# One planner's rule for transfers behind a row of single words, wider weight chunks, and a bound in bfloat16

## The chip, the cores and the metric

The kernel runs on one core of one Trainium2 chip. What counts is the device time of one execution in microseconds, the median of several executions of the same program. The core has five instruction queues that run side by side, each strictly in its own order: PE (matmuls), DVE (vector), ACT (scalar), POOL (GpSimd) and SP, which here issues all the DMAs. An instruction that waits for a semaphore holds up everything behind it on its queue.

## The reference

Attention of many tokens to few pooled keys, and then a feed-forward layer with the gate h − tanh(h). The keys are pooled 4 × 4 and serve as the values too:

```python
B, N, C = q.shape                       # 4, 12288, 128
kv_pool = kv.reshape(B, H // r, r, W // r, r, C).mean(axis=(2, 4))   # 96 x 8 places: 768 keys a batch
k = v = kv_pool.reshape(B, -1, C) @ w_sr
s = scale * (q @ k.transpose(0, 2, 1))
a = np.exp(s - s.max(-1, keepdims=True))
x = (a / (a.sum(-1, keepdims=True) + 1e-09)) @ v
h = x.reshape(B * N, C) @ w_in          # w_in: 128 x 2048, float64
g = h - np.tanh(h)
out = g @ w_out                         # w_out: 2048 x 128, float64
```

## The kernel before

**Precision.** Nearly all matmuls run in float16, and an operand that needs more bits is split into a high and a low half: `qh`/`ql`, `vt` (two parts), `a` (two parts), `x` (two parts), `wih`/`wil`, `woh`/`wol`, `gh`/`gl`. The float64 weights arrive as pairs of 32-bit words and are turned into float32 by bit operations on DVE and ACT.

**Groups and units.** The 49152 tokens are worked on in 96 groups of 512 tokens (24 to a batch). Attention of a group, `attention(g, …)`, goes through four tiles of 128 tokens. Per tile: six matmuls give the scores `s` (L695), DVE takes the largest, `nm` (L703), ACT the exponential `e` with its sum (L709) and the high half of `a` (L714), POOL the low half (L717), and SP transposes both halves by a DMA into `at` (L721). When all four sums are there, DVE makes their inverse `inv` (L734); `store_row` (L738) writes these 512 numbers to DRAM as single 4-byte words, and `load_row` (L742) reads them back spread over all partitions as `row`; SP waits for the store's landing before that load. Groups 0 and 1 make their row on PE. The values' product `x` (L774, 18 matmuls in six steps) needs all four transposes. DVE then divides by `row` (L787) and splits `x` (L794); a store `xs` of x goes out for a rarely taken other branch.

The feed-forward layer of a group has eight units. Per unit PE computes `h` (`forth`, L814 to L816, six matmuls of 512 columns), ACT tanh and a square (L842, L845), DVE `gg` (L848), POOL `gh` (L852), DVE `gl` (L859), and PE adds to `acc` (`fro`, L820 to L822, six matmuls). After eight units ACT scales `acc` into `o` (L881) and SP stores it (L884). PE works on the scores of one group, the values of the one before it and the units of an earlier one in turn.

**What sets the order.** No engine's order is written out. Every instruction is given to the class `Plan` with a step (a place in the sequence), an engine, an estimated time, and what it reads and writes; `Plan.run` then goes through time, always starts the instruction that can begin first (or, among those that can begin within `SOON`, the one with the lowest step), and the order so found is the order in the program. `SHIFT` moves all instructions of a kind by some steps, `EARLY` whole parts. The estimates are used in this planning only: on the chip, waits are set by semaphores. Three marks for DMAs matter here. `"rows"` is the row store, which notes when it will have landed (10 us later). `"read"` marks loads. A transpose has neither.

**Start and end.** The keys of the first batch arrive in pieces by place (`product_of_place`, L512: float32 matmuls with `wsr`); those of the later batches are pooled by DVE (L501) during the batch before. `words_of` (L303 to L346) turns the weights' words to float32 in chunks of WN = 512 columns, four chunks for each matrix; `weights_in` and `weights_out` scale and split them. The last part, `is_small`, bounds the largest h from the weights' column sums (L950: `of_m` by `aw`, four float32 matmuls of 512 columns) and sets the flag that chooses between this path and the other branch.

Of the kernel before, what the change touches and what calls it, by code (L numbers as in the profile page):

```python
# [20 lines left out]
P = 128  # L21
KB = 64
WN = 512
G = 512
# [40 lines left out]
class Plan:  # L65
# [10 lines left out]
        "divide": 0.1, "exps": -0.64, "forth": 0.58, "fro": 3.75, "g_high": 1.39, "g_low": 0.61,  # L76
        "inverse": 0.06, "largest_score": -1.25, "largest_x": -0.1, "pool": 12.74,
        "q_high": 0.33, "q_low": 0.28, "result": -0.72, "scores": 0.18, "square": -0.48,
        "store": -1.47, "store_row": 3.34, "store_x": 0.33, "tanh": -0.6, "turn_weights": 0.78,
# [42 lines left out]
    def run(self, between):  # L122
# [78 lines left out]
def attention_then_ffn(ctx: ExitStack, tc: tile.TileContext, q, kv, w_sr, w_in, w_out, out):  # L201
# [92 lines left out]
    def words_of(step, load_step, n, kind, out):  # L294
# [3 lines left out]
        sb(words, "words", [P, WN, 2], U32, 4)  # L298
        sb(ym, "ym", [P, 2, WN], F32, 2)

        def load():
            if kind == "i":
                SP.dma_start(out=plan[words], in_=w_in32[:, n * WN : (n + 1) * WN, :])  # L303
            else:
                SP.dma_start(out=plan[words].rearrange("p (t c) two -> p t c two", c=C),
                             in_=w_out32[:, n * (WN // P) : (n + 1) * (WN // P)])

# [41 lines left out]
        plan.op(load_step, "SP", 0.5, load, (), (words,), late=2.0, dma=1.3, dram="read")  # L349
        plan.op(step, "DVE", 0.36, top, (words,), (Y,), port=True)  # L350
        plan.op(step, "ACT", 0.6, size, (Y,), (M,))
        plan.op(step, "DVE", 0.7, bottom, (M, Y), (Y,), port=True)
        plan.op(step, "DVE", 0.36, shift, (Y,), (M,), port=True)
        plan.op(step, "DVE", 0.7, upper, (Y, M), (part,), port=True)
        plan.op(step, "DVE", 0.36, power, (part,), (Y,), port=True)
        plan.op(step, "DVE", 0.7, lower, (words, Y), (M,), port=True)
        plan.op(step, "POOL", 1.5, add, (part, M), (part,))

    def weights_in(step):

        wa = "wa"
        sb(wa, "at", [P, F], F32, 2)
        for n in range(NW):
            words_of(step, step - 46 + 3 * n, n, "i", (wa, slice(n * WN, (n + 1) * WN)))
        by, back = wis[:, 1:2], wis[:, 0:1]

        def largest(n):
            V.tensor_reduce(out=top4[:, n : n + 1], in_=plan[wa][:, n * WN : (n + 1) * WN],
                            op=ALU.max, axis=AX.X, apply_absolute_value=True)

        def power():
            V.tensor_reduce(out=by, in_=top4, op=ALU.max, axis=AX.X)
            power_of_two(by, back, 2.0**-100)

        def high(n):
            sl = slice(n * WN, (n + 1) * WN)
            A.activation(out=wih[:, sl], in_=plan[wa][:, sl], func=AF.Copy, scale=by)

        def low(n):
            sl = slice(n * WN, (n + 1) * WN)  # L380
            V.scalar_tensor_tensor(out=wil[:, sl], in0=plan[wa][:, sl], scalar=by, in1=wih[:, sl],
                                   op0=ALU.mult, op1=ALU.subtract)

        top4 = const.tile([P, NW], F32, name="top4")
        plan.tile("top4", "top4", 1, lambda: None)
        for n in range(NW):
            plan.op(step, "DVE", 0.67, partial(largest, n), ((wa, n * WN),), (("top4", n),))
        plan.op(step, "DVE", 0.8, power, ("top4",), ("wis",))
        for n in range(NW):
            plan.op(step, "ACT", 0.6, partial(high, n), ((wa, n * WN), "wis"), (("wih", n),))  # L390
            plan.op(step, "DVE", 0.7, partial(low, n), ((wa, n * WN), "wis", ("wih", n)),
                    (("wi", n),), port=True)

    def weights_out(step):
# [9 lines left out]
        places = [("wb.0", 0), ("wb.1", 0), ("wb.2", 0), ("wb.2", WN)][:NW]  # L404
        assert NW <= 4
# [14 lines left out]
        for n in range(NW):  # L420
# [3 lines left out]
            sb(aw, "aw", [P, WN], F32, 2)  # L424
            plan.op(step + n, "ACT", 0.62, partial(sizes, n, aw), ((key, at),), (aw,), late=0.1)
            plan.op(step + n, "PE", 1.0, partial(sums, n, aw), (aw, "ident"), ("sum.o",), late=0.2,
# [39 lines left out]
        for n in range(NW):  # L466
            key, at = places[n]
            s = step + NW + 1 + n
            plan.op(s, "DVE", 0.7, partial(scaled, n), ((key, at), "sum.o"), ((key, at),))
            plan.op(s, "ACT", 0.6, partial(high, n), ((key, at),), (("woh", n),))  # L470
            plan.op(s, "DVE", 0.7, partial(low, n), ((key, at), ("woh", n)), (("wol", n),), port=True)
            plan.op(s, "ACT", 0.6, partial(small, n), (("woh", n),), (("wo", n),))
# [17 lines left out]
    def keys(b, s0):  # L490
# [25 lines left out]
        if b:  # L516
            gap, cut = 6, 4
            sb(kvp, "kvp", [P, K], F32, 1)
            for j in range(K // KB):
# [3 lines left out]
                        dram="read", after=("unit", *divmod(int(s) - 8, UN)))  # L523
# [41 lines left out]
        def size():  # L565
            back, by = plan[vs][:, 0:1], plan[vs][:, 1:2]
            V.tensor_reduce(out=by, in_=sums(), op=ALU.max, axis=AX.XY, apply_absolute_value=True)
            power_of_two(by, back, 2.0**-80)
            V.tensor_scalar(out=back, in0=back, scalar1=1.0 / W, scalar2=None, op0=ALU.mult)
# [47 lines left out]
        plan.op(s0, "DVE", 2.0, size, (pk,), (vs, scale_q))  # L617
        plan.op(s0, "ACT", 0.92, values_high, (pk, vs), ((vt, 0),))
        plan.op(s0, "DVE", 0.95, values_low, (pk, vs, (vt, 0)), ((vt, 1),))
# [21 lines left out]
    def attention(g, s0):  # L641
# [36 lines left out]
        plan.op(s0 - 8, "SP", 0.4, load_q, (), (qs,), late=2.0, dma=0.65, dram="read")  # L678
# [85 lines left out]
        else:  # L764
# [3 lines left out]
                    dram="read")  # L768
# [40 lines left out]
        plan.op(s2 + 2, "SP", 0.5, store_x, (x2,), (f"xs.{g}",), late=2.0, dma=0.8)  # L809
# [14 lines left out]
    def feed_forward(g, s0):  # L824
# [62 lines left out]
        plan.op(s0 + UN + 2, "SP", 0.5, store, (o,), (), late=3.0, dma=0.65)  # L887
# [5 lines left out]
    def is_small(step):  # L893
        for k, shape in (("m", [P, 2]), ("of_m", [P, P]), ("tops", [P, F // G]), ("by", [P, B]),
                         ("fits", [P, B + 1])):
            sb(k, k, shape, F32, 1)
        plan.tile("stat", "stat", 1, lambda: None)
# [17 lines left out]
        def weigh():  # L915
            V.tensor_tensor(out=plan["fits"][:, 0:B], in0=stat[:, 0:B], in1=plan["by"], op=ALU.mult)
            V.tensor_reduce(out=plan["m"][:, 0:1], in_=plan["fits"][:, 0:B], op=ALU.max, axis=AX.X)
            V.tensor_scalar(out=plan["of_m"], in0=ones, scalar1=plan["m"][:, 0:1], scalar2=1.001,
# [22 lines left out]
        for n in range(F // G):  # L941
            aw, p = f"aw.{n}", f"p.{n}"
            sb(aw, "row", [P, G], F32, 2)
# [12 lines left out]
            plan.op(step + n, "PE", 1.1, total, (aw, "of_m"), (p,), late=0.2, wide=True)  # L956
# [129 lines left out]
    weights_in(-LEAD - 1 + early("weights_in", 0.0))  # L1086
# [69 lines left out]
```

## Time and profile before

| | |
|---|---|
| median of 3 runs | 2847.41 us (2844.72 to 2848.29) |
| profiled execution | 2846.34 us, its span 2844.6 us, mean granted clock 0.997 |
| PE busy | 2795.4 us, 98% of the span |
| DVE busy | 2685.2 us, 94% |
| ACT busy | 2593.7 us, 91% |
| POOL busy | 1368.2 us, 48% |
| DMA | 285 MB, mean 100 GB/s; 665168 of 736420 packets under 512 B |
| SP's waits for a row store's landing (L742) | 493.0 us in 78 waits, longest 8.3 us |

"Busy" is the time in which an engine has an instruction in work. A row such as `PE x L774 <- DMA at<-a: 9.0, 3, 5.3` reads: PE, before instructions of line 774 that write x, sat idle until DMAs from a to at had landed; 9.0 us in all, three times, 5.3 the longest. In a row for one line the numbers behind the count are the shortest, median and longest duration in ns, then the start of the first and the last in us; a line "DMA to landing" under it is the time from issue to landing. In a row of a stretch stand its bounds and length, then busy us (and instructions) of PE, PEld, DVE, ACT and POOL, the granted PE clock, the share of the DMA engines, and GB/s. A matmul's duration is longer than its distance to the next one, since matmuls overlap.

### The profile page before, as it was taken

Reading aid. Unit: us, or ns where it says so; the run is one execution under the profiler, and the core shown is the slowest. Engines: PE = TensorE matmul, PEld = TensorE weight load, DVE = VectorE, ACT = ScalarE, POOL = GpSimd, SP = SyncE. Lnnn points to the kernel's source line nnn. Section 1 sums busy time; section 2 is a strip of 40 time slices with the busy share of each in tenths; the row PEclk is TensorE's granted clock in tenths of the full one; section 3 lists DMA queues with packets and bytes.
Section 4 is the critical chain, followed back from the end, with each engine's and each line's share of the span. In section 5 each row is a group of like instructions: output and inputs, shape, how many; then the busy total and the mean of one; then the engine's idle time right before and its main releaser. Section 6 shows DMA issues by size and latency. Waiting matters only on the chain. (4 is left out here: it accounts for less than half of the span.)

```text
span 2844.6 us, 39535 instructions
## 1 busy us (share of the span) xinstructions
PE 2795.4 (98%) x13380; PEld 1318.0 (46%) x13380; DVE 2685.2 (94%) x3212; ACT 2593.7 (91%) x3307; POOL 1368.2 (48%) x1069
## 2 busy tenths in 40 slices
PE   7899999999999999999999999999999999999998
PEld 3444444444444444444444444444444444444443
DVE  7989999999999999999999999999999999999998
ACT  5989999999999999999999999999999999999986
POOL 3444544444544544444545454444444454545442
PEclk9999999999999999999999999999999999999999
DMA  8445466565444446655544544666454445444430
GB/s 231 80 81 99 88 113 111 116 119 90 97 87 100 87 99 107 119 112 118 91 97 89 97 89 100 116 115 118 98 98 86 98 87 100 87 100 86 97 78 28
DMA packets 736420, 285.01 MB, mean 100 GB/s; under 512 B 665168, under 2 KB 692944, under 8 KB 736208
## 3 DMA queue, kind: packets, MB, share of 16 engines
q1 hardware_dynamic: 736208, 282.41, 50.8%
q8 instruction: 106, 1.74, 0.4%
q14 instruction: 106, 0.87, 0.2%
HBM read 79.23 MB, written 50.52 MB: 46 GB/s over the span
## 5 line engine op out<-in xcount | busy, mean ns | idle before, releaser
L852 POOL TENSOR_SCALAR gh<-gg 128x1024 f16<-128x1024 f32 x672 | 723.7, 1077 | 1237.3 <-DVE gl L859 676.5
L848 DVE SCALAR_TENSOR_TENSOR gg<-h,by_batch,t 128x1024 f32<-128x1024 f32 x768 | 983.1, 1280 | 87.7 <-ACT t L845 31.4
L859 DVE SCALAR_TENSOR_TENSOR gl<-gh,gg 128x1024 f16<-128x1024 f16 x768 | 1005.6, 1310 | 8.0 <-POOL gh L852 2.2
L842 ACT ACTIVATE t<-h,by_batch 128x1024 f32<-128x1024 f32 x768 | 850.3, 1107 | 124.7 <-PE h L816 118.3
L845 ACT ACTIVATE t<-t 128x1024 f32<-128x1024 f32 x768 | 811.3, 1056 | 21.2
L717 POOL TENSOR_TENSOR a<-e,a 128x768 f16<-128x768 f32 x384 | 633.6, 1650 | 209.4 <-ACT t L845 84.5
L814 PE MATMUL h<-x,wih 128*128 128x512 f16 x1536 | 582.1, 379 | 13.8 <-DVE gg L848 12.6
L822 PE MATMUL acc<-gl,wos 128*128 128x512 f16 x1536 | 582.4, 379 | 0.3 <-DVE gl L859 0.3
L820 PE MATMUL acc<-gh,woh 128*128 128x512 f16 x1536 | 582.5, 379 | 0.0
L821 PE MATMUL acc<-gh,wol 128*128 128x512 f16 x1536 | 582.4, 379 | 0.0
L815 PE MATMUL h<-x,wih 128*128 128x512 f16 x1536 | 582.0, 379 | 0.2 <-DVE x L794 0.2
L816 PE MATMUL h<-x,wil 128*128 128x512 f16 x1536 | 582.0, 379 | 0.0
L774 PE MATMUL x<-at,vv 128*128 128x512 f16 x1728 | 467.8, 381 | 9.2 <-DMA at<-a 9.0
L709 ACT ACTIVATE e<-s,nm 128x768 f32<-128x768 f32 x380 | 340.3, 896 | 58.5 <-DVE nm L705 56.1
L703 DVE TENSOR_REDUCE nm<-s 128x1 f32<-128x768 f32 x380 | 361.0, 950 | 20.9 <-PE s L695 20.8
L714 ACT CAST a<-e 128x768 f16<-128x768 f32 x384 | 315.5, 822 | 3.0
L695 PE MATMUL s<-vt,qh 128*128 128x384 f16 x1520 | 311.0, 327 | 6.9 <-DVE vt L578 4.8
L774 PEld LDWEIGHTS <-vv 128*128 128x128 f16 x1728 | 169.3, 98 | 212.7 <-DMA at<-a 7.4
L814 PEld LDWEIGHTS <-wih 128*128 128x128 f16 x1536 | 150.1, 98 | 186.9 <-DVE gg L848 18.2
L815 PEld LDWEIGHTS <-wih 128*128 128x128 f16 x1536 | 150.0, 98 | 184.9 <-issue 21.8
L822 PEld LDWEIGHTS <-wos 128*128 128x128 f16 x1536 | 150.4, 98 | 181.4 <-issue 0.5
L816 PEld LDWEIGHTS <-wil 128*128 128x128 f16 x1536 | 150.1, 98 | 181.7 <-issue 0.5
(136 smaller groups left out, 1774.2 us busy)
## 6 DMA issues: line engine op xcount, KB each, us to landing
qs<-in_q_dram SPq DMA_DIRECT2D x96, 256.0 KB, 2.7
xs<-x SPq DMA_DIRECT2D x96, 256.0 KB, 2.4
out_dram<-o SPq DMA_DIRECT2D x96, 256.0 KB, 2.4
row<-sums_row SPq DMA_DIRECT2D x94, 256.0 KB, 4.5
kc<-in_kv_dram SPq DMA_DIRECT2D x36, 512.0 KB, 4.4
at<-a SPq DMA_TRANSPOSE x384, 4.0
kc<-in_kv_dram SPq DMA_DIRECT2D x8, 384.0 KB, 7.4
words<-in_moe_w_in_dram SPq DMA_DIRECT2D x4, 512.0 KB, 8.4
```

The source lines that it names most:

```text
L717: return PL.tensor_tensor(out=plan[a][:, 1], in0=plan[e], in1=plan[a][:, 0], op=ALU.subtract)
L774: PE.matmul(out=plan[x], lhsT=l, rhs=r, start=(n == 0 and k == 0), stop=(n == KT - 1 and k == 2))
L814: PE.matmul(out=h, lhsT=wih[:, fs], rhs=xh, start=True, stop=False)
L815: PE.matmul(out=h, lhsT=wih[:, fs], rhs=xl, start=False, stop=False)
L816: PE.matmul(out=h, lhsT=wil[:, fs], rhs=xh, start=False, stop=True)
L820: PE.matmul(out=acc, lhsT=woh[:, fs], rhs=gh, start=(f == 0), stop=False)
L822: PE.matmul(out=acc, lhsT=wos[:, fs], rhs=gl, start=False, stop=(f == FT - 1))
L842: A.activation(out=plan[t], in_=plan[h], func=AF.Tanh, scale=node)
L845: A.activation(out=plan[t], in_=plan[t], func=AF.Square)
L848: V.scalar_tensor_tensor(out=plan[gg], in0=plan[h], scalar=weight, in1=plan[t], op0=ALU.mult, op1=ALU.mult)
L852: return PL.tensor_scalar(out=plan[gh], in0=plan[gg], scalar1=1.0 / LOW, scalar2=1.0, op0=ALU.mult, op1=ALU.mult)
L859: return V.scalar_tensor_tensor(out=plan[gl], in0=plan[gh], scalar=-LOW, in1=plan[gg], op0=ALU.mult, op1=ALU.add)
```

## The change

Five edits.

1. **The planner.** A transfer marked `"wait"` isn't started on SP before the last row store is planned to have landed. The mark is given to the loads of weights' words, keys and q, to `load_row`, and to the stores of x and of the result. Before, only loads were affected, and only by a later landing. Transposes are free of the rule in both. The tables of shifts are new.
2. **WN from 512 to 1024.** Two chunks for each weight matrix instead of four, each loaded by two DMAs of 512 KB; the ring of `words` has two buffers instead of four, all chunks of `w_out` lie in buffers of the keys (`kc`).
3. **`size` of the keys in two.** The split of `vt` needs only the first part of the key's scale.
4. **The bound in bfloat16.** `of_m` and `aw` of `is_small` become bfloat16, with a margin of 1.02 for 1.001.
5. **Keys first.** The first key tile is loaded before the first words, and all words of `w_out` behind the last keys.

```diff
-WN = 512
+WN = 1024
...
     SHIFT = {
...
-        "values": 1.09, "weight_high": 0.78, "weight_low": 0.56, "x_high": 0.78, "x_low": -7.03,
+        "values": 2.47, "weight_high": 0.78, "weight_low": 1.15, "x_high": 0.53, "x_low": -5.72,
...
-    EARLY = {"attention 0": -2.7, "attention 1": -3.6, "attention 2": -2.1, "attention 3": -5.1, "weights_in": -1.6, "weights_out": 9.5}
-    SOON = 0.184
+    EARLY = {"attention 0": -6.1, "attention 1": -4.0, "attention 2": -4.0, "attention 3": -9.3, "weights_in": -11.5, "weights_out": 12.3}
+    SOON = 0.126
...
                         held = free.get("port", 0.0) if self.ops[i][5] else 0.0
+                        if self.ops[i][8] == "wait":
+                            held = free.get("rows", 0.0)
...
             if dma:
-                landed = free.get("rows", 0.0) if dram == "read" else 0.0
-                free["dma"] = max(free.get("dma", 0.0), now + us, landed) + dma
+                free["dma"] = max(free.get("dma", 0.0), now + us) + dma
...
-        sb(words, "words", [P, WN, 2], U32, 4)
+        sb(words, "words", [P, WN, 2], U32, 2)
...
-        plan.op(load_step, "SP", 0.5, load, (), (words,), late=2.0, dma=1.3, dram="read")
-        plan.op(step, "DVE", 0.36, top, (words,), (Y,), port=True)
+        for h in range(2):
+            plan.op(load_step + 3 * h, "SP", 0.45, partial(load, h), (), ((words, h),), late=2.0,
+                    dma=1.3, dram="wait")
+        plan.op(step, "DVE", 0.7, top, (words,), (Y,), port=True)
...
-        sb("wb.0", "o", [P, WN], F32, 2)
-        sb("wb.1", "o", [P, WN], F32, 2)
-        sb("wb.2", "kc", [P, 2 * WN], F32, 5)
+        for n in range(NW):
+            sb(f"wb.{n}", "kc", [P, WN], F32, 5)
...
-        plan.op(s0, "DVE", 2.0, size, (pk,), (vs, scale_q))
-        plan.op(s0, "ACT", 0.92, values_high, (pk, vs), ((vt, 0),))
+        plan.op(s0, "DVE", 1.6, size, (pk,), (vs,))
+        plan.op(s0, "DVE", 0.35, size_by_window, (vs,), ((vs, 0), scale_q))
+        plan.op(s0, "ACT", 0.92, values_high, (pk, (vs, 1)), ((vt, 0),))
...
             plan.op(s1, "SP", 0.5, load_row, (f"dram.{g}",), (row,), late=3.2, dma=0.65,
-                    dram="read")
+                    dram="wait")
...
-        plan.op(s2 + 2, "SP", 0.5, store_x, (x2,), (f"xs.{g}",), late=2.0, dma=0.8)
+        plan.op(s2 + 2, "SP", 0.5, store_x, (x2,), (f"xs.{g}",), late=2.0, dma=0.8, dram="wait")
...
-        plan.op(s0 + UN + 2, "SP", 0.5, store, (o,), (), late=3.0, dma=0.65)
+        plan.op(s0 + UN + 2, "SP", 0.4, store, (o,), (), late=2.0, dma=0.65, dram="wait")
...
+        sb("of_m", "of_m", [P, P], BF16, 1)
...
-            sb(aw, "row", [P, G], F32, 2)
+            sb(aw, "qj", [P, G], BF16, 1)
...
-            plan.op(step + n, "PE", 1.1, total, (aw, "of_m"), (p,), late=0.2, wide=True)
+            plan.op(step + n, "PE", 0.22, total, (aw, "of_m"), (p,), late=0.2)
```

**How it moves instructions.** First SP in the start of the program, around the row store of group 3. In these rows `at<-a` is a transpose, `sums_row<-inv` the row store, `row<-sums_row` the row's load, `xs<-x` the store of x, `qs` a load of q. Before:

```order
L721 DMA_TRANSPOSE at<-a 128x12x128 x3
L742 DMA row<-sums_row 128x512
L721 DMA_TRANSPOSE at<-a 128x12x128
L802 DMA xs<-x_768 256x1x512
L721 DMA_TRANSPOSE at<-a 128x12x128
L738 DMA sums_row<-inv 128x4x1
L802 DMA xs<-x_858 256x1x512
L662 DMA qs<-in_q_dram 128x512
L742 DMA row<-sums_row 128x512
```

And after:

```order
L729 DMA_TRANSPOSE at<-a 128x12x128 x3
L750 DMA row<-sums_row 128x512
L810 DMA xs<-x_669 256x1x512
L729 DMA_TRANSPOSE at<-a 128x12x128
L746 DMA sums_row<-inv 128x4x1
L729 DMA_TRANSPOSE at<-a 128x12x128
L750 DMA row<-sums_row 128x512
L810 DMA xs<-x_757 256x1x512
```

Before, the fourth transpose of group 3 (the single one behind the first `xs<-x`) stands ahead of the group's row store. After, the row store stands between the third and the fourth.

Then SP at the first change of batch, around the row store of group 25. Before:

```order
L721 DMA_TRANSPOSE at<-a 128x12x128
L742 DMA row<-sums_row 128x512
L721 DMA_TRANSPOSE at<-a 128x12x128
L802 DMA xs<-x_7213 256x1x512
L721 DMA_TRANSPOSE at<-a 128x12x128
L662 DMA qs<-in_q_dram 128x512
L721 DMA_TRANSPOSE at<-a 128x12x128
L738 DMA sums_row<-inv 128x4x1
L721 DMA_TRANSPOSE at<-a 128x12x128
```

And after:

```order
L729 DMA_TRANSPOSE at<-a 128x12x128 x3
L810 DMA xs<-x_7131 256x1x512
L670 DMA qs<-in_q_dram 128x512
L746 DMA sums_row<-inv 128x4x1
L729 DMA_TRANSPOSE at<-a 128x12x128 x2
L892 DMA out_dram<-o 128x512
L750 DMA row<-sums_row 128x512
```

Here too the fourth transpose stood ahead of the store; after, it is the first of the two behind it. The same holds in groups 49 and 73, where the next batches begin.

DVE at the same place, from the largest score `nm` of group 25's last tile to the inverse of its sums. Before:

```order
L703 TENSOR_REDUCE nm<-s 128x1
L705 TENSOR_SCALAR nm<-nm 128x1
L798 TENSOR_REDUCE most_x<-x_7213 128x1
L859 SCALAR_TENSOR_TENSOR gl<-gh,gg 128x1024
L670 SCALAR_TENSOR_TENSOR ql<-qs,by_batch,qh 128x512
L848 SCALAR_TENSOR_TENSOR gg<-h,by_batch,t 128x1024
L734 TENSOR_REDUCE inv<-sums_all 128x4
L735 RECIPROCAL inv<-inv 128x4
```

And after:

```order
L711 TENSOR_REDUCE nm<-s 128x1
L713 TENSOR_SCALAR nm<-nm 128x1
L806 TENSOR_REDUCE most_x<-x_7131 128x1
L802 TENSOR_TENSOR x_7131<-xf,x_7131 128x512
L867 SCALAR_TENSOR_TENSOR gl<-gh,gg 128x1024 x2
L678 SCALAR_TENSOR_TENSOR ql<-qs,by_batch,qh 128x512
L856 SCALAR_TENSOR_TENSOR gg<-h,by_batch,t 128x1024 x2
L711 TENSOR_REDUCE nm<-s 128x1
L713 TENSOR_SCALAR nm<-nm 128x1
L742 TENSOR_REDUCE inv<-sums_all 128x4
L743 RECIPROCAL inv<-inv 128x4
```

x_low, a second gl, a second gg and the next tile's `nm` now stand ahead of the inverse. On PE, between the last score matmul of group 25 and its first value matmul, stood 24 matmuls of scores, 18 of values and 114 of units; after, 12, 18 and 60. In group 3 it was 6, 18 and 84; after, 15 of values, 12 of units and eight small ones of the weights' scale, and the first `fro` of the program stands behind the values of group 3 (before, ahead of them).

More of the change, by code (lines that the diff above doesn't have):

```diff
@@ L297, in words_of, with load @@
         a, at = out
-        sb(words, "words", [P, WN, 2], U32, 4)
+        sb(words, "words", [P, WN, 2], U32, 2)
         sb(ym, "ym", [P, 2, WN], F32, 2)
-        def load():
+        def load(h):
+            half = WN // 2
+            at = slice(n * WN + h * half, n * WN + (h + 1) * half)
+            to = plan[words][:, h * half : (h + 1) * half]
             if kind == "i":
-                SP.dma_start(out=plan[words], in_=w_in32[:, n * WN : (n + 1) * WN, :])
+                SP.dma_start(out=to, in_=w_in32[:, at, :])
             else:
-                SP.dma_start(out=plan[words].rearrange("p (t c) two -> p t c two", c=C),
-                             in_=w_out32[:, n * (WN // P) : (n + 1) * (WN // P)])
+                SP.dma_start(out=to.rearrange("p (t c) two -> p t c two", c=C),
+                             in_=w_out32[:, at.start // P : at.stop // P])
         def y(dt=F32):
@@ L348, in words_of, with weights_in @@
         Y, M, part = (ym, "y"), (ym, "m"), (a, at.start)
-        plan.op(load_step, "SP", 0.5, load, (), (words,), late=2.0, dma=1.3, dram="read")
-        plan.op(step, "DVE", 0.36, top, (words,), (Y,), port=True)
[L351 to L359, printed above, removed]
+        for h in range(2):
+            plan.op(load_step + 3 * h, "SP", 0.45, partial(load, h), (), ((words, h),), late=2.0,
+                    dma=1.3, dram="wait")
+        plan.op(step, "DVE", 0.7, top, (words,), (Y,), port=True)
+        plan.op(step, "ACT", 1.06, size, (Y,), (M,))
+        plan.op(step, "DVE", 1.24, bottom, (M, Y), (Y,), port=True)
+        plan.op(step, "DVE", 0.7, shift, (Y,), (M,), port=True)
+        plan.op(step, "DVE", 1.24, upper, (Y, M), (part,), port=True)
+        plan.op(step, "DVE", 0.7, power, (part,), (Y,), port=True)
+        plan.op(step, "DVE", 1.24, lower, (words, Y), (M,), port=True)
+        plan.op(step, "POOL", 2.6, add, (part, M), (part,))
+    def weights_in(step, first):
         wa = "wa"
@@ L363, in weights_in @@
         for n in range(NW):
-            words_of(step, step - 46 + 3 * n, n, "i", (wa, slice(n * WN, (n + 1) * WN)))
+            words_of(step, first + 1 + 6 * n, n, "i", (wa, slice(n * WN, (n + 1) * WN)))
         by, back = wis[:, 1:2], wis[:, 0:1]
@@ L386, in weights_in @@
         for n in range(NW):
-            plan.op(step, "DVE", 0.67, partial(largest, n), ((wa, n * WN),), (("top4", n),))
+            plan.op(step, "DVE", 1.2, partial(largest, n), ((wa, n * WN),), (("top4", n),))
         plan.op(step, "DVE", 0.8, power, ("top4",), ("wis",))
         for n in range(NW):
-            plan.op(step, "ACT", 0.6, partial(high, n), ((wa, n * WN), "wis"), (("wih", n),))
-            plan.op(step, "DVE", 0.7, partial(low, n), ((wa, n * WN), "wis", ("wih", n)),
+            plan.op(step, "ACT", 1.08, partial(high, n), ((wa, n * WN), "wis"), (("wih", n),))
+            plan.op(step, "DVE", 1.24, partial(low, n), ((wa, n * WN), "wis", ("wih", n)),
                     (("wi", n),), port=True)
@@ L403, in weights_out @@
         plan.tile("col", "col", 1, lambda: None)
-        places = [("wb.0", 0), ("wb.1", 0), ("wb.2", 0), ("wb.2", WN)][:NW]
-        assert NW <= 4
+        places = [(f"wb.{n}", 0) for n in range(NW)]
         def chunk(n):
@@ L423, in weights_out @@
             words_of(step + n, step + n - 4, n, "o", (key, slice(at, at + WN)))
-            sb(aw, "aw", [P, WN], F32, 2)
-            plan.op(step + n, "ACT", 0.62, partial(sizes, n, aw), ((key, at),), (aw,), late=0.1)
-            plan.op(step + n, "PE", 1.0, partial(sums, n, aw), (aw, "ident"), ("sum.o",), late=0.2,
+            sb(aw, "aw", [P, WN], F32, 1)
+            plan.op(step + n, "ACT", 1.08, partial(sizes, n, aw), ((key, at),), (aw,), late=0.1)
+            plan.op(step + n, "PE", 1.9, partial(sums, n, aw), (aw, "ident"), ("sum.o",), late=0.2,
                     wide=True)
@@ L468, in weights_out @@
             s = step + NW + 1 + n
[L469 to L472, printed above, removed]
+            plan.op(s, "DVE", 1.2, partial(scaled, n), ((key, at), "sum.o"), ((key, at),))
+            plan.op(s, "ACT", 1.05, partial(high, n), ((key, at),), (("woh", n),))
+            plan.op(s, "DVE", 1.2, partial(low, n), ((key, at), ("woh", n)), (("wol", n),), port=True)
+            plan.op(s, "ACT", 1.05, partial(small, n), (("woh", n),), (("wo", n),))
     plan.tile("wih", "wih", 1, lambda: None)
@@ L522, in keys @@
                 plan.op(s - 6, "SP", 0.5, partial(load, j, KB, key), (), (key,), late=2.0, dma=1.3,
-                        dram="read", after=("unit", *divmod(int(s) - 8, UN)))
+                        dram="wait", after=("unit", *divmod(int(s) - 8, UN)))
                 for k in range(cut):
```

20 lines of the change are left out of this document (11 added, 9 removed).

## The prediction

> **What bounds the kernel now.** I read the page first, then the waits of PE by stretch, the busy time by stretch, the DMA issues on SP, and last single instructions around the waits. From the page:
>
> ```profile
> span 2844.6 us, 39535 instructions
> PE 2795.4 (98%) x13380; PEld 1318.0 (46%) x13380; DVE 2685.2 (94%) x3212; ACT 2593.7 (91%) x3307; POOL 1368.2 (48%) x1069
> ...
> GB/s 231 80 81 99 88 113 111 116 119 90 97 87 100 87 99 107 119 112 118 91 97 89 97 89 100 116 115 118 98 98 86 98 87 100 87 100 86 97 78 28
> ```
>
> TensorE is the bound: 2844.6 − 2795.4 leaves 49.2 us of PE idleness, and only that can be won without taking PE work away. DVE, at 94%, is a close second. PE's waits, first up to 160 us, then in the middle from 300 to 2750 us (total us, times, longest):
>
> ```profile
> PE x L774 <- DMA at<-a: 9.0, 3, 5.3
> PE s L512 <- DMA t<-in_kv_dram: 7.7, 1, 7.7
> PE h L814 <- DVE gg L848: 5.7, 17, 0.5
> ```
>
> The third row is the whole wait of 2450 us: the middle has 5.7 us to give, about 1.9 at each of its three changes of batch. The start holds the rest, and there the values' product (L774) waits for transposed weights `at`. Busy time by stretch (each engine's busy us, then the granted clock):
>
> ```profile
> 50.00:100.00 50.00, 38.83 (x186) 19.17 (x185) 42.05 (x75) 46.57 (x79) 28.37 (x20) 0.93 0.72 132
> 100.00:150.00 50.00, 48.65 (x232) 22.43 (x230) 48.49 (x53) 44.15 (x56) 23.51 (x18) 1.00 0.35 62
> ```
>
> From 100 us on both PE and DVE are nearly full, so whatever PE loses there isn't made up later.
>
> **The row of single words.** `store_row` (L738) writes 512 single words; a transpose (L721) usually lands 4 us after its issue. Landing lines, of the row stores and then of all transposes (min/median/max):
>
> ```profile
> DMA to landing us min/median/max: 7.7/9.0/13.6
> DMA to landing us min/median/max: 3.6/4.0/11.9
> ```
>
> The long transposes are those issued just behind a row store. First group 4 (its last scores on PE, row store, transpose, first values), then a group of the steady state:
>
> ```profile
> L695 PE MATMUL s<-vt,ql x2: 326/326/326, 133.6 to 133.7; 128*128 128x384 f16 x2
> L738 SPq DMA_DIRECT2D sums_row<-inv x1: 833/833/833, 141.0 to 141.0; - x1
> L721 SPq DMA_TRANSPOSE at<-a x1: 7079/7079/7079, 144.4 to 144.4; - x1
> DMA to landing us min/median/max: 10.4/10.4/10.4
> L774 PE MATMUL x<-at,vv x3: 607/634/634, 154.9 to 155.7; 128*128 128x512 f16 x3
> ...
> L695 PE MATMUL s<-vt,ql x2: 326/326/326, 282.4 to 282.5; 128*128 128x384 f16 x2
> L738 SPq DMA_DIRECT2D sums_row<-inv x1: 389/389/389, 290.7 to 290.7; - x1
> L721 SPq DMA_TRANSPOSE at<-a x1: 1422/1422/1422, 291.9 to 291.9; - x1
> DMA to landing us min/median/max: 10.7/10.7/10.7
> ```
>
> Landings: 154.8 and 302.6, so 13.8 and 11.9 us behind the store's issue and 20.9 and 19.9 behind the end of the scores. With nothing ahead of it the same step is short, in group 3 and, at a change of batch, in group 25:
>
> ```profile
> L695 PE MATMUL s<-vt,ql x2: 326/326/326, 86.9 to 87.1; 128*128 128x384 f16 x2
> L721 SPq DMA_TRANSPOSE at<-a x1: 1435/1435/1435, 98.4 to 98.4; - x1
> DMA to landing us min/median/max: 3.7/3.7/3.7
> ...
> L721 SPq DMA_TRANSPOSE at<-a x1: 1452/1452/1452, 783.4 to 783.4; - x1
> DMA to landing us min/median/max: 3.7/3.7/3.7
> ```
>
> What matters is whether PE has other work queued between a group's last scores and its first values. I count it from PE's order: 0.22 us for a matmul of 512 columns (row of the tail below), 0.16 for one of 384. In the steady state of before that is 32.4 us, against 19.9: hidden. In group 4 it is 15.5 against 20.9, and the difference, 5.4, is the longest wait of L774, 5.3. This one place shows the whole mechanism.
>
> **Part 1, the planner.** The new rule holds loads and stores while a row is on its way, but not transposes, which are what PE waits for; a transpose is still priced at 4.75 us after its start (1.45 + 1.2 + 2.1). With the new tables the work queued on PE becomes, for groups 2 to 5, 10.2, 7.9, 14.9 and 17.5 us (before 14.2, 23.3, 15.5, 30.4); for groups 25 and 26, and likewise at the other two changes, 18.8 and 16.8 (before 32.4 both). In the steady state it stays at 24.9 or more: hidden by that work. In all of these, SP has the row store ahead of the group's last transpose (before, of these groups, only in 2, 4 and 5). The durations on DVE between a score and its row store, from the groups of 55 to 150 us:
>
> ```profile
> L848 DVE SCALAR_TENSOR_TENSOR gg<-h,by_batch,t 128x1024 f32<-128x1024 f32 x19 | 24.2, 1279 | 1.1 <-ACT t L845 0.2
> L859 DVE SCALAR_TENSOR_TENSOR gl<-gh,gg 128x1024 f16<-128x1024 f16 x17 | 21.9, 1293 | 0.2 <-POOL gh L852 0.2
> L703 DVE TENSOR_REDUCE nm<-s 128x1 f32<-128x768 f32 x14 | 13.3, 951 | 3.4 <-PE s L695 3.4
> L794 DVE TENSOR_TENSOR x<-xf,x 128x512 f16<-128x512 f32 x4 | 3.4, 853 | 0.0
> L798 DVE TENSOR_REDUCE most_x<-x 128x1 f32<-128x512 f16 x4 | 2.7, 680 | 0.5 <-ACT x L791 0.5
> L670 DVE SCALAR_TENSOR_TENSOR ql<-qs,by_batch,qh 128x512 f16<-128x512 f32 x3 | 2.3, 752 | 0.0
> L342 DVE SCALAR_TENSOR_TENSOR ym<-words,ym 128x512 f32<-128x512 uint32 x3 | 2.1, 693 | 0.1
> ```
>
> Group 3. Walking the new order with these durations I put its last scores at 88.6 (before 87.4). Then nm (1.1 with its sign), two gg (2.6) and the inverse (0.3) put the row store at about 93.5 and, 11.9 later, the transpose at 105.5. The values (18 × 0.22) and one unit's six matmuls, which now stand ahead of the first `fro`, bring that to 105.5 + 5.2 = 110.7. Without the hold, DVE would let it start at 103.6 (nm, and 13.6 us of rows up to the last `wol`). The cost is 7. The first `fro` started here before:
>
> ```profile
> L820 PE MATMUL acc<-gh,woh x1536: 376/379/634, 99.3 to 2837.3; 128*128 128x512 f16 x192
> ```
>
> 62.3 us of matmuls stand ahead of it before and 66.2 after, so PE was 37.0 us behind its work there, and would be 37.4 without the hold and 44.5 with it. Group 4: 20.9 against 14.9 instead of 15.5, +0.6. Group 5: 19.9 against 17.5, +2.4. A stall of this size also lowers the clock. After the waits of 2.5 and 5.3 us, and in an undisturbed stretch:
>
> ```profile
> PE x L774 <- DMA at<-a: 2.5, 1, 2.5
> ...
> 55.00:60.00 5.00, 4.46 (x13) 1.72 (x12) 1.55 (x5) 4.92 (x11) 4.28 (x3) 0.50 1.04 189
> 155.00:160.00 5.00, 5.00 (x15) 2.01 (x14) 2.83 (x4) 1.62 (x2) 1.64 (x1) 0.55 0.85 207
> 160.00:165.00 5.00, 5.00 (x25) 2.25 (x23) 2.89 (x3) 3.36 (x4) 0.00 (x0) 1.00 0.09 17
> ```
>
> 15 matmuls where 25 fit: 10 × 0.2 = 2.0 us, which I add once for group 5. The start: 7 + 0.6 + 2.4 + 2.0 = +12.
>
> The Trainium skill ("TensorE: Matmul & The Clock Gate", Part 1: The HAM clock gate) has the clock halved after about 3.4 us of idleness, which would spare group 5's stall and one in each batch change, some 2 us apiece; the 0.50 behind a wait of 2.5 us says otherwise, so the added 2.0 stays.
>
> Group 25. DVE now has x_low, most_x, two gl, ql, two gg and the next nm between nm and the inverse: 0.85 + 0.68 + 2.59 + 0.75 + 2.56 + 1.1 + 0.3 = 8.8, with nm itself 9.9. The store goes at about 10.8 behind the scores and the transpose lands 11.9 later, 22.7 against 18.8: +3.9. Group 26: 19.9 against 16.8, +3.1, less as DVE catches up in the first stall; I take 2. Plus one loss of clock, 2.0, minus the 1.9 that PE waited there anyway: +6 for each change of batch, +18 in all. Bounds: −5.7 (no stall, and the old waits gone) to +30.
>
> **Part 2, 1024 columns.** On DVE some 32 instructions fewer. Row L342 against row L848, twice the width: 693 × 2 − 1279 = 107 ns each, 3.4 us of DVE before the first `fro`; that is in the 103.6. **Part 3**, the split `size`: two tiny operations off the way, 0.3 us at most, inside the same wait. **Part 5, keys first**: the first key no longer queues behind 512 KB of words; at the 231 GB/s of the page's first slice that is some 2.3 us of the 7.7. But DVE now has both chunks of `wil` ahead of the first group's ql, 2 × 1.28 us (L848's width), so I leave the first scores where they are: 0, between −2.3 and 0. The words of `w_out`, now behind the last keys, come later by what two key loads take; DVE has the first groups' scores to do meanwhile.
>
> **Part 4, bound in bfloat16.** One pair of L950 in the tail's chain, and one ordinary matmul:
>
> ```profile
> 2799.88 0.22 PE acc L821
> ...
> 2823.00 0.86 PE x L950 x2
> ```
>
> Four pairs at 0.86, replaced by four matmuls at 0.22: −2.6, on PE's path (PE waits little there); between −2.6 and 0, since DVE is full up to the last gl.
>
> **Sum.** Profiled execution 2846.3 + 12 + 18 − 2.6 = 2873.7; it lies 1.1 under the median of the runs, 2847.4, so 2874.8, and with the caught-up side a little larger than I can count, 2873 (+0.9%).
>
> **Rivals.** (a) Faster: in the new places the transpose isn't held, or lands early enough. For it: in group 2 of before the transpose is issued 4.5 us behind the store, which lands 8.8 us after its own issue, and PE doesn't wait, so a store that goes early costs less; and DVE, not PE, may pace both places.
>
> ```profile
> L738 SPq DMA_DIRECT2D sums_row<-inv x1: 399/399/399, 76.3 to 76.3; - x1
> ...
> L721 SPq DMA_TRANSPOSE at<-a x1: 2659/2659/2659, 80.8 to 80.8; - x1
> ```
>
>  Then the waits of 5.3 with its 2.0 of clock and the tail go: 2846.3 − 7.3 − 2.6 + 1.1 = 2837.5. It decides if the transposes of groups 3 and 25 land under 14 us after their scores. Against it stand both landings above 10 us. Here the Trainium skill ("DMA: Bandwidth & Descriptors", Queues, rings and completion order) speaks for (a): data descriptors carry no barrier, and a later transfer may finish before an earlier one; by that the time would be (a)'s, and landings of 10.4 and 10.7 against 3.7 disagree. (b) The start stalls, the changes of batch don't, since DVE's extra pooling gives PE's queue its own delay: 2846.3 + 12 − 2.6 + 1.1 = 2857. (c) The change doesn't do what it says: what the rule holds back on SP was hidden before and is now, and new stalls equal the old ones: 2843 to 2852.
>
> **How the numbers follow.** Forecast 0.45 (own range 2862 to 2888: batch changes at +3 to +10), (a) 0.27, (b) 0.17, (c) 0.11. A measurement here can tell 0.2% from no change (2841.7 to 2853.1). Faster 0.27, same 0.11, slower 0.62. The range runs from (a), 2837, to the forecast's upper end, 2888; about 0.1 is left out on each side.
>
> **What would show it.** Right: PE waits at the values for `at` near 100, 130 to 160, 770 and 800 us, and likewise 700 us later twice; transposes of 10 us and more behind row stores there; the granted clock low right behind; first `fro` at 108 or later. The first key's wait near 5.7 and the first scores no earlier; the bound's matmuls four at 0.22. Wrong: PE's waits for `at` under 9 us in all, first `fro` before 104, or PE full from 750 to 850. What I trust least is the walk of DVE up to 88.6 and 22.7: each us there moves the sum by one, or three.

## The result

The changed kernel took 2876.14 us in the median of four runs (2875.07 to 2876.76), the kernel before 2846.73 beside it: a ratio of 1.0107, 95% interval 1.0093 to 1.012. It is slower, by 29.4 us. First the page of the changed kernel:

```profile
span 2874.8 us, 39147 instructions
PE 2803.3 (98%) x13375; PEld 1315.6 (46%) x13376; DVE 2672.0 (93%) x3180; ACT 2584.6 (90%) x3295; POOL 1382.0 (48%) x1065
```

The span grew by 30.2 us. PE's idleness went from 49.2 to 71.5 us, and PE's busy time rose by 7.9 although it has four matmuls fewer to do. Part of that is a slower clock: the mean granted clock of the two profiled executions is 0.995 against 0.997. Another part is waiting that doesn't show as idleness. Here are both kernels from the first `forth` of group 11 to that of group 78, before and after, with the same number of matmuls and the clock at 1.00 in both:

```profile
398.00:2327.70 1929.70, 1923.06 (x9266) 905.46 (x9265) 1850.45 (x2228) 1793.91 (x2282) 943.09 (x737) 1.00 0.54 102
408.40:2358.00 1949.60, 1929.92 (x9266) 904.14 (x9265) 1856.12 (x2228) 1788.48 (x2279) 949.65 (x738) 1.00 0.54 101
```

Of the 19.9 us that this stretch is longer, 13.0 are idleness and 6.9 are busy time. A matmul of 512 columns is in work for 379 ns and the next one starts 216 ns after it, so a gap shorter than the difference counts as busy. In this stretch PE starts a unit's or a score's first matmul 0.1 to 0.3 us late 61 times in the changed kernel (11.3 us in all) and 21 times before (4.3). DVE and ACT each have less to do over the whole program (13 and 9 us). PE's waits, up to 170 us, then up to 2780, then the rest:

```profile
PE x L782 <- DMA at<-a: 9.7, 3, 4.5
PE s L703 <- ACT qh L675: 6.8, 1, 6.8
PE s L703 <- ACT e L717: 5.6, 6, 2.0
PE s L516 <- DMA t<-in_kv_dram: 5.3, 1, 5.3
PE x L782 <- issue: 5.2, 1, 5.2
...
PE h L822 <- DVE gg L856: 7.0, 22, 0.7
PE x L782 <- DMA at<-a: 6.0, 4, 1.7
PE acc L830 <- DVE gl L867: 4.0, 3, 1.4
...
PE h L822 <- DVE gg L856: 2.5, 2, 1.6
PE acc L828 <- POOL gh L860: 1.6, 2, 1.4
PE acc L830 <- DVE gl L867: 1.5, 3, 0.7
```

L782 is the values' product (L774 before), L703 the scores, L830 the last part of `fro`. A fourth row of the second block, `x <- gl` with 1.3 us in one wait, is left out here. Apart from its waits for gg the second block is new: the kernel before had 6.3 us of waits for gg there and 0.2 for x. A row with `issue` names no releaser; the one of 5.2 us stands ahead of the values of group 4, whose last transpose was issued 1.6 us behind the row store. Followed group by group (the first `forth` of each), the changed kernel is 10.4 us behind at group 11, 16.5 at group 30, 23.7 at group 54 and 30.3 at group 78; its end is 30.2 behind. The loss arises in the start and around the three changes of batch.

The places that the prediction named, in order of time: group 3's last scores, its row store, its fourth transpose, its first values; then the row store, the transpose and the first values of group 25:

```profile
L703 PE MATMUL s<-vt,ql x2: 527/528/528, 88.0 to 88.3; 128*128 128x384 f16 x2
L746 SPq DMA_DIRECT2D sums_row<-inv x1: 394/394/394, 92.7 to 92.7; - x1
L729 SPq DMA_TRANSPOSE at<-a x1: 1287/1287/1287, 93.8 to 93.8; - x1
L782 PE MATMUL x<-at,vv x8: 607/634/635, 101.0 to 104.0; 128*128 128x512 f16 x8
...
L746 SPq DMA_DIRECT2D sums_row<-inv x1: 370/370/370, 764.8 to 764.8; - x1
L729 SPq DMA_TRANSPOSE at<-a x1: 1457/1457/1457, 766.3 to 766.3; - x1
L782 PE MATMUL x<-at,vv x6: 377/378/379, 775.4 to 776.4; 128*128 128x512 f16 x6
```

Both transposes sit behind a row store, and the values start 8.3 and 10.6 us after that store's issue. Group 25's wait of 1.3 us stands under `x <- gl` in the profile; it goes with the 16-byte stores below, so it is counted here as a wait for the transpose. The granted clock (last but two columns) behind the wait in group 3, and at the batch change:

```profile
100.00:105.00 5.00, 4.01 (x10) 1.49 (x11) 5.00 (x5) 3.60 (x4) 0.00 (x0) 0.50 0.26 49
755.00:760.00 5.00, 3.65 (x18) 1.60 (x17) 4.93 (x8) 4.90 (x7) 0.58 (x1) 1.00 0.55 125
775.00:780.00 5.00, 4.64 (x23) 2.27 (x24) 3.66 (x4) 4.49 (x7) 2.52 (x2) 1.00 0.75 184
```

It falls to half with a wait of 4.5 us, and stays at 1.00 with those of 1.1 to 1.4 us.

### The profile page after: what moved, and what is told of

Same layout as the page of the kernel before. It is cut to its first block, busy times and chain, and to the rows that moved or that the text cites. A ratio compares the mean times of both kernels' runs of the same rounds, so it can differ in the third digit from the quotient of the medians.

```text
span 2874.8 us, 39147 instructions
## 1 busy us (share of the span) xinstructions
PE 2803.3 (98%) x13375; PEld 1315.6 (46%) x13376; DVE 2672.0 (93%) x3180; ACT 2584.6 (90%) x3295; POOL 1382.0 (48%) x1065
## 5 line engine op out<-in xcount | busy, mean ns | idle before, releaser
L860 POOL TENSOR_SCALAR gh<-gg 128x1024 f16<-128x1024 f32 x672 | 738.9, 1100 | 932.9 <-DVE gl L867 353.5
L853 ACT ACTIVATE t<-t 128x1024 f32<-128x1024 f32 x768 | 811.4, 1057 | 22.4
L822 PE MATMUL h<-x,wih 128*128 128x512 f16 x1536 | 582.2, 379 | 12.6 <-DVE gg L856 10.2
L830 PE MATMUL acc<-gl,wos 128*128 128x512 f16 x1536 | 582.7, 379 | 5.6 <-DVE gl L867 5.6
L782 PE MATMUL x<-at,vv 128*128 128x512 f16 x1728 | 463.7, 382 | 22.3 <-DMA at<-a 15.6
L703 PE MATMUL s<-vt,qh 128*128 128x384 f16 x1520 | 310.3, 327 | 12.9 <-ACT qh L675 6.8
L782 PEld LDWEIGHTS <-vv 128*128 128x128 f16 x1728 | 169.5, 99 | 224.7 <-issue 21.2
L828 PEld LDWEIGHTS <-woh 128*128 128x128 f16 x1536 | 150.5, 98 | 185.2 <-issue 8.0
L822 PEld LDWEIGHTS <-wih 128*128 128x128 f16 x1536 | 150.1, 98 | 185.5 <-DVE gg L856 18.3
L830 PEld LDWEIGHTS <-wos 128*128 128x128 f16 x1536 | 150.4, 98 | 181.6 <-issue 0.6
```

Source lines behind the costliest of these rows:

```text
L782: PE.matmul(out=plan[x], lhsT=l, rhs=r, start=(n == 0 and k == 0), stop=(n == KT - 1 and k == 2))
L822: PE.matmul(out=h, lhsT=wih[:, fs], rhs=xh, start=True, stop=False)
L828: PE.matmul(out=acc, lhsT=woh[:, fs], rhs=gh, start=(f == 0), stop=False)
L830: PE.matmul(out=acc, lhsT=wos[:, fs], rhs=gl, start=False, stop=(f == FT - 1))
L853: A.activation(out=plan[t], in_=plan[t], func=AF.Square)
L860: return PL.tensor_scalar(out=plan[gh], in0=plan[gg], scalar1=1.0 / LOW, scalar2=1.0, op0=ALU.mult, op1=ALU.mult)
```

## The experiments

Theory A: transposes are held by the row of single words, and the new order leaves PE too little else at those places. Theory B: the new order itself costs PE the time, whatever a store takes. Theory C: the wide chunks or the keys' order cost the start. The twelve runs, each with the kernel before on the same chip; lines with the same time of before belong together, and the three times belong to three chips:

| kernel | median us | ratio to before, 95% | before |
|---|---|---|---|
| changed, 16-byte row stores | 2858.56 | 1.0042 [1.0025, 1.0059] | 2846.01 |
| before, 16-byte row stores | 2838.84 | 0.9974 [0.9964, 0.9983] | 2846.01 |
| changed, fourth transpose first | 2864.28 | 1.0058 [1.0041, 1.0074] | 2846.01 |
| parts 2 to 5 alone | 2894.45 | 1.0166 [1.0149, 1.0183] | 2846.01 |
| before, group 4's transpose first | 2836.26 | 0.9961 [0.9948, 0.9975] | 2846.83 |
| part 4 alone | 2847.29 | 1.0001 [0.9992, 1.001] | 2846.83 |
| part 1 alone | 2893.96 | 1.0162 [1.0147, 1.0178] | 2846.83 |
| changed, 16-byte store in group 3 | 2889.92 | 1.0145 [1.0129, 1.016] | 2846.83 |
| changed, once more | 2892.86 | 1.0164 [1.0147, 1.0181] | 2846.55 |
| 16-byte store in group 3, again | 2890.11 | 1.0155 [1.0138, 1.0172] | 2846.55 |
| 16-byte stores at batch changes | 2873.56 | 1.0095 [1.0078, 1.0112] | 2846.55 |
| changed, forth and fro set back | 2864.10 | 1.0063 [1.0046, 1.008] | 2846.55 |

**The store without single words, order unchanged.** In both kernels:

```diff
-            SP.dma_start(out=sums_row[g].rearrange("t p -> p t"), in_=plan[inv])
+            SP.dma_start(out=sums_row[g].rearrange("t p -> (t p)").rearrange("(p t) -> p t", t=TT), in_=plan[inv])
```

> The changed kernel in its own order, but each row store writes its 512 numbers as 128 pieces of 16 bytes instead of 512 single words; the row is read back in that order, so its numbers reach other tokens than they belong to. Theory A (transposes are held by the row of single words, and the new order leaves PE little else there): transposes behind a row store land in 4 to 6 us, PE's waits for them fall from some 21 us (9.7 and 5.2 up to 170 us, 6.0 later) to under 5, the clock stays up after 85 us, and the time falls by 15 to 24: 2852 to 2861. Theory B (the new order itself costs PE the time, on DVE, ACT and POOL, whatever a store takes): 2872 to 2877.

> The kernel before with the same 16-byte row stores (its row too reaches other tokens). Theory A: only group 4's wait of 5.3 us and the slow clock behind it go: 2839 to 2842. Theory B: the store's landing plays no part: 2845 to 2848.

Landings in the changed kernel, of row stores with single words (the profile has the landing of only 4 of the 94), of row stores in 16-byte pieces (all 94), and of all transposes with the latter:

```profile
DMA to landing us min/median/max: 8.1/9.7/11.4
...
DMA to landing us min/median/max: 1.4/2.1/4.1
...
DMA to landing us min/median/max: 3.6/3.8/5.7
```

The holding is gone: no transpose takes over 5.7 us, where 10.7 was the longest of the 54 on record. The kernel before shows the holding in more places, since the profile has 288 of its transposes. All 58 that were issued less than 6 us behind a row store took 6.1 us or more, 10.0 in the median. Of the 71 issued up to 3 us ahead of one, 70 took at most 4.6; the one left is the 11.9 of the prediction's landing line, which landed 0.2 us before the store did. PE's waits from 170 to 2790 us, with 16-byte stores in the changed kernel, are these two alone:

```profile
PE h L822 <- DVE gg L856: 6.9, 24, 0.7
PE acc L830 <- DVE gl L867: 4.1, 3, 1.4
```

The changed kernel gains 17.6 us against the first measurement (2876.1 to 2858.6), within A's range. The changed kernel itself was not run on this chip, and on another it takes 2892.9 (below). The kernel before gains 7.2 (2846.0 to 2838.8), as A said to within 0.2 us. But 2858.6 − 2838.8 = 19.7 us between the two kernels remain with nothing held. Of the 29.4 first measured, the holding's net share is then 9.7, and two thirds are the order's own: A and B both hold, B for the larger part. By place: the start of the changed kernel (to group 11) falls from 408.4 to 398.3, that of before from 398.0 to 389.2. So in the start the holding costs both kernels about the same (10.1 and 8.8), and the order 9.1. Each change of batch gains 2.7 us by the store and stays some 4 above before. Between groups 11 and 78 that makes 12.2 us with nothing held, of which 5.4 are idleness and 6.8 busy time, at a clock of 1.00 and with the same number of matmuls.

What the order costs in the start is spread over small waits. PE's waits up to 170 us with nothing held, first some that are longer in the changed kernel's order, then their counterparts in that of before:

```profile
PE s L703 <- ACT qh L675: 6.8, 1, 6.8
PE s L703 <- ACT e L717: 5.0, 5, 2.0
PE x L782 <- ACT a L722: 2.0, 1, 2.0
PE x L782 <- DVE xf L795: 1.9, 1, 1.9
PE x L759 <- DVE xf L795: 1.2, 1, 1.2
...
PE s L695 <- DVE vt L578: 4.8, 1, 4.8
PE s L695 <- ACT e L709: 2.5, 4, 1.2
PE x L751 <- DVE xf L787: 0.4, 1, 0.4
```

These rows differ by 9.2 us, but others go the other way (the first key's wait is 4.7 us in place of 7.0). Up to group 11 PE's idleness differs by 5.7 of the 9.1 us; the other 3.4 are busy time, with next to the same clock, and where they arise was not followed.

**Group 3 alone.** The same edit `if g == 3`. It was run twice, the second time beside the changed kernel itself.

> The changed kernel in its own order, with the 16-byte row store in group 3 alone (that group's row reaches other tokens). With 16-byte stores in all groups the start was 10.1 us shorter. Theory A, each wait by itself: group 3's wait of 4.5 us and the slow clock behind it (4.5 to 7 us in all) go and group 4's stays, 2869 to 2872. If one wait saved is given back at the next (group 4 then waits longer): 2873 to 2877.

> The same kernel as before with 16-byte stores in group 3 alone, now beside the changed kernel on one chip. Theory A: 3 to 7 us under the changed kernel of this chip (group 3's wait of 4.5 and part of the slow clock). If a wait saved is given back at the next: within 2 us of it.

The first result, 2889.9, lies above everything expected, and in places that the edit doesn't touch. The changed kernel itself then took 2892.86 there:

> The changed kernel unchanged, beside the next three on one chip, because the run with 16-byte stores in group 3 alone came out 14 us above the changed kernel's time, in places that the edit doesn't touch (each change of batch 2.5 to 3 us longer, row stores landing in 10.1 us in the median against 9.7). If landings of the row stores differ from chip to chip and the new order passes the difference on, this kernel varies with the chip: 2876 where they land in 9.7, some 2890 to 2897 where they land in 10.1. If the edit itself did it: 2875 to 2877.

Beside it the edit in group 3 brings 2.7 us, less than A's 3 to 7, and 2.0 of that stand before the edit can act (group 3's last scores end at 89.8 for 91.8 us). PE's waits from 84 to 170 us, of the changed kernel (groups 2 and 3 in the first row, 4 in the second) and with the edit (4, then 2):

```profile
PE x L782 <- DMA at<-a: 9.3, 2, 4.9
PE x L782 <- issue: 6.2, 1, 6.2
...
PE x L785 <- issue: 5.7, 1, 5.7
PE x L785 <- DMA at<-a: 4.4, 1, 4.4
PE acc L442 <- DVE kc L457: 3.1, 1, 3.1
```

The 4.9 in group 3 falls to 1.0, and 3.1 comes up at once: PE turns the weights' column scale (L442), for which DVE has not yet scaled `w_out` (L457). Group 3's wait is given back at the next ones. The run with 16-byte stores at the batch changes (below) settles what it costs, for its start is the changed kernel's own on the same chip: the first `forth` of group 1 begins at 119.0 us and that of group 11 at 409.9, with the edit in group 3 and without it. Alone it is worth nothing.

**The changed kernel once more.** Beside these runs the kernel before takes 2846.0 to 2846.8, as ever; the changed one took 2876.1 first and 2892.9 now, each within 2.5 us of its median. The landing of the row stores in the second profile of the changed kernel, and PE's waits from 170 to 2780 us there:

```profile
DMA to landing us min/median/max: 8.9/10.3/12.0
...
PE x L782 <- DMA at<-a: 10.2, 5, 2.9
PE h L822 <- DVE gg L856: 8.1, 20, 1.6
PE acc L830 <- DVE gl L867: 4.0, 3, 1.4
PE x L782 <- DVE gl L867: 2.4, 1, 2.4
```

The stores' line rests on the same four stores as above, but the transposes say the same: the 13 that took over 6 us in the first profile land 1.1 us later in this one. PE's waits at the changes of batch are 12.6 us for 7.3 (the row `x <- gl` is the same place: values of group 25), and the matmuls behind three of the longer ones run at half the clock. Before's order has 32 us of other work queued there, and doesn't pass later landings on: in the run with part 4 alone, in that order, the stores land in 9.7 us in the median (9.0 in the first profile of before), and PE waits for no transpose behind 170 us. Whether the later landings belong to the chip or to the hour isn't told apart by these runs.

**The batch changes alone.** The 16-byte store `if g >= NG and g % NG in (1, 2)`.

> The changed kernel with 16-byte row stores in groups 25, 26, 49, 50, 73 and 74 alone (those rows reach other tokens): the holding at the changes of batch is gone, the start keeps it. Theory A, with 16-byte stores in all groups having shortened each change of batch by 2.5 us: 7 to 10 us under the changed kernel of this chip, more (to 16) where the stores land later; the waits for gl at these places (1.3 to 1.5 each) stay. Theory B: within 2 us of it.

19.3 us under the changed kernel of the same chip, more than the 16 expected at most. 16 of them lie between groups 11 and 78, 5.3 for each change of batch, and 2.9 in the start, which the edit doesn't touch; the waits for gl stay at 4.1 in all. So the holding cost 2.7 us at each change of batch in the first measurement and 5.3 in this one. If the order's own 19.7 us are the same on this chip, which was not measured, the holding's net share is 9.7 of 29.4 there and some 27 of 46.3 here (2892.9 − 2846.6, less 19.7).

**Transpose first.** The planner starts a group's row store only behind its fourth transpose (`behind` is a new argument of `op`, which makes an instruction follow the beginning of another):

```diff
             plan.op(s1, "SP", 0.5, store_row, (inv,), (f"dram.{g}",), late=10.0, dma=0.8,
-                    dram="rows")
+                    dram="rows", behind=("turn", g, TT - 1))
```

> The changed kernel with one more rule for its planner: a group's row store is begun behind the group's fourth transpose. Nothing else is changed, but the planner's order moves with it (PE's work between group 25's scores and values about doubles). Theory A: group 3 to 5's and the batch changes' waits for transposes go, some 15 to 25 us: 2850 to 2861. Theory B: 2870 to 2880.

2864.3, 11.9 less than first measured (the changed kernel wasn't run on this chip); the waits for `at` behind 170 us are gone. A's places were right, its sum too high: this order has waits of its own in the start (6.8 us for the scaled `w_out`). Since the whole order moved, this run doesn't show the holding's cost by itself.

**One move in the kernel before.** The same rule `if g == 4`, in the kernel before. On SP the row store goes behind `xs` and the transpose, and the row's load behind the next transpose; no other engine's order changes.

> The kernel before with one move on SP: in group 4 alone the row store goes behind the group's fourth transpose instead of ahead of it; PE, DVE, ACT and POOL keep their order. Theory A (a transpose behind the row store is held): the transpose lands at 148 instead of 154.8, PE's wait of 5.3 us there and the slow clock behind it go, the row comes some 5 us later and nobody waits: 2838 to 2841, faster than both. If the row is then late for the division, the gain is only 2 to 4. Theory B: no change, 2845 to 2848.

2836.3, 10.6 us less than before, a little under what A expected and the lowest time of this study. Between 140 and 170 us, PE's one wait of before was the first row here; with the move it waits for nothing there, and the clock stays at 1.00 (the stretch behind it, 15 matmuls before):

```profile
PE x L774 <- DMA at<-a: 5.3, 1, 5.3
...
155.00:160.00 5.00, 5.00 (x26) 2.44 (x25) 4.93 (x5) 4.94 (x7) 1.04 (x1) 1.00 0.96 101
```

Right behind group 4 everything is 7.4 us further ahead than at group 3: the wait of 5.3 us, and 2 of slow matmuls. One more microsecond was there before group 4, and the rest isn't accounted for.

**Part 4 alone.**

> The kernel before with part 4 alone, the bound from bfloat16 factors (the order moves in the last units only). By the prediction's term 2.6 us less, 2843 to 2844.5. By the rival reading of the changed kernel's end (DVE and POOL pace the last units, and PE's saved time turns into waits for gg, gh and gl): within 1 us of before, 2845.5 to 2847.5.

2847.3: nothing. PE's waits from 2790 us on, of this kernel (before it had 0.4, 0.4 and 0.3):

```profile
PE acc L822 <- DVE gl L859: 2.1, 2, 1.5
PE h L814 <- DVE gg L848: 1.7, 2, 1.5
PE acc L820 <- POOL gh L852: 0.2, 1, 0.2
```

The time saved on PE came back as 2.9 us more of waits, and all but 0.2 us of them are for DVE.

**Part 1 alone, and parts 2 to 5 alone.**

> The kernel before with part 1 alone, the planner's rule, marks and tables. Theory A with the order's own cost as a second part: the changes of batch cost as in the changed kernel, 6 to 7 us each, and the start stalls in group 3 (least work queued there) and 4: 2870 to 2884. If the wide chunks and keys first are what cost the start its 10 us (theory C), the start is as before and the time 2862 to 2867.

> The changed kernel with the planner's rule and all tables of the kernel before: wide chunks, split size, bfloat16 bound and keys first alone. Theories A and B (the planner's part is what costs): 2840 to 2850. Theory C (the wide chunks or the keys' order cost the start its 10 us): 2855 or more.

2894.0 and 2894.5: each half alone is about as slow as or slower than both together. Part 1 alone lies above its 2870 to 2884; it ran beside the first run with the edit in group 3, where the changed kernel's order takes some 2890. Its start takes 407.9 us to group 11, against 398.0 before, so the start is lost without the wide chunks and without keys first. Parts 2 to 5 alone lie far above the 2840 to 2850 of A and B, and their start takes 405.5: it loses 7.5 us without the planner's part. So theory C doesn't explain the start by itself, and it isn't refuted either: each half alone costs most of what both together cost in the start. Most of the loss of parts 2 to 5 lies elsewhere, 33.9 us between groups 11 and 78, where no weight is prepared any more and PE waits 9.5 us for `o` and 2.9 for `a`. PE's order differs from before's there too: the old tables give this list of instructions another order throughout. What parts 2, 3 and 5 are worth in a fitting order was not measured.

**More between forth and fro.** `"forth": 0.58, "fro": 3.75` in the changed kernel.

> The changed kernel with two entries of its tables set back, forth to 0.58 and fro to 3.75, which puts fro further behind forth. For theory B's share (some 4 us at each change of batch and the end, that stay with 16-byte stores: PE waits for gl and gh because fro follows too closely): waits of fro for gl and gh (7.2 us in all) fall under 2, and the time by 4 to 12. If the order's cost lies elsewhere: within 3 us, either way.

28.8 us less than the changed kernel beside it, far over the expectation, and for another reason. PE's waits from 170 to 2780 us:

```profile
PE h L822 <- DVE gg L856: 8.1, 26, 1.2
PE acc L830 <- DVE gl L867: 4.1, 3, 1.4
PE acc L828 <- ACT o L889: 0.7, 2, 0.3
PE x L782 <- DVE xf L795: 0.6, 1, 0.6
```

The waits for gl, which were to go, stay. The waits for `at`, 10.2 and 2.4, are gone: in this order group 25's transpose precedes the store again, and group 26 has more work queued. Group 4's wait fell from 6.2 to 1.7. Why fro waits 1.4 us for gl at each change of batch stays open.

## Why the prediction was right, and where it was not

The forecast was 2873 and the measured time 2876.1, slower as forecast. By its steps:

- **The mechanism** (a transpose behind the row of single words lands when that is through, and PE waits if too little work is queued) is shown: with 16-byte stores in the same order the long landings go in both kernels, and of PE's waits for `at` one of 1.5 us and one of 2.5 are left; the move in group 4 takes 5.3 us and the slow clock out of the kernel before. Rival (a) needed landings under 14 us behind the scores. Group 25's values began 22.4 us behind theirs (753.0 to 775.4), the walk had 22.7. Group 3's began 12.2 us behind (88.8 to 101.0), so by its own sign (a) held in that half; PE waited 4.5 us all the same, since only 7.9 us of work were queued. Of the Trainium skill's statement that a later transfer may finish before an earlier one ("DMA: Bandwidth & Descriptors", Queues, rings and completion order), the runs showed no case here: no transpose on record landed before a row store of single words that was issued ahead of it.
- **Group 3, +7**: this term failed. The transpose was there at 101 instead of 105.5, 8.3 us behind the store's issue and not 11.9, and the wait of 4.5 hid another, for the scaled `w_out`. (The walk's own terms, 88.6 + 1.1 + 2.6 + 0.3, make 92.6 and not 93.5; the store went at 92.7.) The walk put the first `fro` without the hold at 103.6; with 16-byte stores it came at 106.4, and with the hold at 108.7. That is 2.3 us in place of 7, and with the hold taken out of group 3 alone nothing was gained by group 11: that whatever PE loses there isn't made up later was wrong for this wait.
- **Group 4, +0.6**: the landing was right (20.9 against 15.5 before, 21.1 against 14.9 now), but the wait didn't grow (5.3 and 5.2). **Group 5, +2.4 and 2.0 of clock**: failed; the values began 17.3 us behind the scores without a wait. Group 2, which the sum left out, waited 3.3 us (1.2 before).
- **The start, +12**, measured +10.4, was right in size for the wrong reason: with nothing held the two starts still differ by 9.1 us. The waits for q's split, exp and the division that the experiment with nothing held shows are a part of them; 3.4 us aren't idleness at all. Keys first gave 2.4 us at the first key and lost 2.0 of it at q's split: near the 0 of the sum.
- **Changes of batch, +6 each**, measured 6.1, 7.2 and 6.6. The waits were 1.1 to 1.7 for `at` in a group instead of 3.9 and 2, the clock stayed at 1.00, so its 2.0 weren't due, and the 1.9 of waits for gg didn't go. Some 4 of each are the order's own, for which the sum had no term.
- **The bound, −2.6**: failed. Its bound of 0 was the value; the sentence that gave it (DVE is full up to the last gl) was the one to follow.
- **The clock**: a wait of 4.5 us halved it, those of up to 1.7 at the changes of batch did not. The length of one wait doesn't decide it in between. In the kernel before it fell within a wait of 2.5 us, while with 16-byte stores a wait of 2.5 left it at 1.00; of two waits of 2.4 in the second profile of the changed kernel, one (at 2215.9) lowered it and one (at 780.7) didn't. The limit that the Trainium skill gives ("TensorE: Matmul & The Clock Gate", Part 1: The HAM clock gate), about 3.4 us of idleness, is thus not one of unbroken idleness here; what else counts these runs don't show.

So the sum's terms were too high where PE waits for transposes and had nothing for the order's own cost, and the two errors met: that 2873 came within 3.1 us of 2876.1 is luck. In its later runs the same program took 2892.9, above the forecast's own range to 2888; the sum had no term for stores that land later.

## What to carry to other kernels

Where transfers share a queue, look at what an urgent one stands behind: a store of single words kept the transposes behind it some 6 us longer, and moving it behind one transpose, in one group, was worth 10.6 us. A wait that is taken away shows the next one; only the difference between the two is gained. Compare busy time as well as idleness: gaps shorter than a matmul's overlap count as busy. A planner's tables that fit one list of instructions gave a poor order with another here, and the order that left little queued work passed later landings on to PE.

## What the runs showed that was not expected

- The changed kernel took 2876.1 us in its first runs and 2892.9 in its later ones, while the kernel before took 2846.0 to 2846.8 beside either. The 13 longest transposes of its first profile land 1.1 us later in its second.
- 512 numbers stored as 512 single words landed in 9.0 us in the median in the kernel before (72 of 94 stores on record), as 128 pieces of 16 bytes in 2.1 (94 of 94).
